# A 352-byte tile at the right-hand end of SBUF moves the right-hand pools from 480 to 128 bytes over multiples of 512

## The chip, the cores and the metric

The kernel runs on one core of a Trainium2 chip. The metric is the device time of one execution in microseconds. Before the change three runs took 923.97, 925.14 and 925.65 us, median 925.14. All durations below are from one profiled execution, which took 923.92 us.

## The reference

A linear attention with a decaying state, then two feed-forward nets. What is computed, cut short:

```python
B, H, S, D = 4, 8, 768, 48
for t in range(S):
    cur = einsum('bhd,bhe->bhde', u * k[:, :, t], v[:, :, t])
    y[:, :, t] = einsum('bhd,bhde->bhe', r[:, :, t], state + cur)
    state = w * state + einsum('bhd,bhe->bhde', k[:, :, t], v[:, :, t])
x = y as (3072 tokens, 384)
g = x @ w_gate                              # 384 x 1536
x = (g * sigmoid(g) * (x @ w_val)) @ w_out  # back to 384
h = x @ w_in                                # 384 x 2048
out = (h * tanh(softplus(h))) @ w_out2      # back to 384
```

All of it is in float32.

## The kernel before

**Work and stages.** The 768 steps of time are cut into six chunks j of 128, and a chunk holds 4 batches x 128 = 512 tokens: the width of a matmul. Attention of a chunk gives its x, transposed (features on partitions). Then comes the first net, chunk by chunk: 12 blocks f of 128 hidden features; a *unit* is one (j, f). Chunks 0 and 1 are worked in pairs for the first seven f. Attention of the later chunks is done in small matmuls between the units of the chunk before. The second net runs after that over three pairs p of chunks, with a Strassen-like scheme: in each of 8 steps q, 11 products ("regions") of the inputs named b, t and d with weight tiles w_split, and products of the hidden g with weight tiles v in three passes a, b and c.

**Every large product is split.** An operand in float32 is held as a rounded part hi and the rest lo, and `product` (line 287) issues three matmuls of 512 columns on line 290 with the same result tile:

```python
add(0, hi, start, False)      # weight hi, streamed hi
add(0, lo, False, False)      # weight hi, streamed lo
add(1, hi, False, stop)       # weight lo, streamed hi
```

`lhsT`, the weight tile, is loaded into the array (LDWEIGHTS, the engine PEld of the profile), `rhs` is streamed. A unit of the first net has 18 such matmuls for gate and value (3 feature blocks x 3, twice), in which x_hi or x_lo is streamed against w_split, and 9 for the down product, in which g_hi or g_lo is streamed against w_split. In the second net all ten split inputs b, t, d are streamed against w_split, and g_hi, g_lo against v.

**Pools and places.** Pools are allocated from the left-hand end of SBUF upward, or with `side="right"` from the right-hand end downward. All sizes below are bytes in a partition.

- On the left 16,384 bytes are reserved and four constants take 32 each, so wpool begins at 16,512 = 32 x 512 + 128. w_split tiles have 3,072 bytes, the o, g_hi and g_lo tiles 2,048, so wpool, opool and gpool all lie 128 over multiples of 512. In the second net the b, t, d tiles (tpool) and the v tiles (vpool) are on the left too, at 128 over. Attention's state, scores and rkv_sb lie 0 over.
- On the right are wpool2 (the other w_split tiles), xpool0 and xpool1 (x_hi, x_lo of even and odd chunks), and in the second net gpool2 (g), spool2 (split pairs of g) and vsums. In the built program all of them lie 480 over a multiple of 512.

Which side a weight tile of the first net is on is set by its number n = 3 f + i, with i = 0 for gate, 1 for value, 2 for down (`w_tile`, line 133): n up to 10, and 12 and 13, are in wpool, the rest in wpool2. So gate and value weights of f = 0 to 4 are on the left and those of f = 5 to 11 on the right; down weights of f = 0 to 2 are on the left and of f = 3 to 11 on the right. They stay there for all chunks. Split pairs of the second net go through seven buffers in turn (`split_of`): two in gpool on the left, five in spool2 on the right. In the first pair of chunks the pairs k = 0 and 1 (step q = 0) and 7 are on the left, 2 to 6 on the right.

**Order.** Nothing is planned by a scheduler here: instructions stand in the order in which the code issues them (`manual_schedule`), each engine works its own in order, and tiles are guarded by semaphores.

Of the kernel before, what the change touches and what calls it, by code (L numbers as in the profile page):

```python
# [16 lines left out]
P = 128  # L17
# [62 lines left out]

W_KEPT = 13


@with_exitstack
def tile_decay_attention_then_two_ffns(
# [17 lines left out]
        return ap.bitcast(F32)  # L103


    right = ExitStack()
    wpool = ctx.enter_context(tc.tile_pool(name="wpool", bufs=W_KEPT))
    wpool2 = right.enter_context(
# [1410 lines left out]
```

## Time and profile before

| | before |
|---|---|
| median of 3 runs | 925.14 us (923.97 to 925.65) |
| the profiled execution's own time | 923.92 us |
| its span, first to last instruction | 922.2 us |
| TensorE matmul (PE) busy | 911.9 us, 99% |
| TensorE weight load (PEld) busy | 734.7 us, 80% |
| VectorE (DVE) busy | 613.5 us, 67% |
| ScalarE (ACT) busy | 436.4 us, 47% |
| GpSimd (POOL) busy | 171.2 us, 19% |
| DMA | 164.24 MB, 178 GB/s on average |
| mean granted TensorE clock | 0.998 |

Matmuls overlap in the records: one lasts about 390 ns, but the next begins some 230 ns after it. The step from one start to the next is what a stream of them costs, and it is read from the chain of work (a piece of n matmuls in so many us) or from start times in the timeline. The stages: up to about 40 us loads and attention of the first chunks; 40 to 560 us the first net with attention of the later chunks in between, of which chunks 0 and 1 up to about 160 us; from 560 us the second net.

### The profile page before, as it was taken

The numbers are of one execution on the slowest core, as the hardware profiler recorded it, in microseconds if no ns is written. First come the engines' busy times: TensorE is split into PE (matmuls) and PEld (weight loads), VectorE is DVE, ScalarE is ACT, GpSimd is POOL, SyncE is SP. The second block draws the span as 40 slices with busy tenths as digits, with TensorE's granted clock in tenths as the row PEclk, the third lists the DMA queues.
The fourth block names the chain that finished last, engine by engine and source line by source line (L and its number), as shares of the span: only waits on it lengthen the run. The fifth ranks groups of instructions, "written<-read, shape, count | busy, mean of one in ns | idle before, by whom it ended". The sixth has DMA issues, their size and how long they took to land.

```text
span 922.2 us, 14893 instructions
## 1 busy us (share of the span) xinstructions
PE 911.9 (99%) x5625; PEld 734.7 (80%) x5625; DVE 613.5 (67%) x1108; ACT 436.4 (47%) x867; POOL 171.2 (19%) x162
## 2 busy tenths in 40 slices
PE   9999999999999999999999999999999999999997
PEld 6878877777788778878888888888888888888885
DVE  8898888545778676733324645658876487775586
ACT  6765543323333443321123346656665565655454
POOL 4100202566555555442000100000000000000000
PEclk9999999999999999999999999999999999999999
DMA  8454732435676766540004648967844558545264
GB/s 316 154 148 125 240 91 82 144 104 180 197 217 211 257 204 203 176 151 30 24 34 143 189 149 285 362 231 258 302 162 160 179 168 303 203 164 166 72 195 145
DMA packets 78600, 164.24 MB, mean 178 GB/s; under 512 B 7616, under 2 KB 36672, under 8 KB 78528
## 3 DMA queue, kind: packets, MB, share of 16 engines
q1 hardware_dynamic: 78096, 162.50, 53.5%
q0 software_dynamic: 432, 0.79, 0.5%
q8 instruction: 44, 0.72, 0.3%
q14 instruction: 28, 0.23, 0.1%
HBM read 126.82 MB, written 36.44 MB: 177 GB/s over the span
## 4 chain that ended last, share of the span: by engine, by line
PE 96%; DVE 2%; DMA 1%; issue 0%; ACT 0%; DVEq 0%
PE mm L290 41%; PE acc L290 27%; PE at L290 19%; PE at L579 3%; PE at L530 2%; PE mm L530 1%; PE at L556 1%; PE at L612 1%; PE acc L488 0%; DMA v<-w2c 0%; PE at L548 0%; PE at L652 0%; DVE o L723 0%; DVE g_lo L731 0%; PE acc L398 0%
## 5 line engine op out<-in xcount | busy, mean ns | idle before, releaser
L290 PE MATMUL mm<-x_hi,w_split 128*128 128x512 f32 x858 | 283.6, 396 | 1.0 <-DVE w_split L230 1.0
L290 PEld LDWEIGHTS mm<-x_hi,w_split 128*128 128x128 f32 x858 | 161.0, 188 | 39.2 <-DVE w_split L230 1.5
L290 PE MATMUL mm<-x_lo,w_split 128*128 128x512 f32 x429 | 168.2, 392 | 0.1
L723 DVE TENSOR_TENSOR o<-mm,o 128x512 f32<-128x512 f32 x72 | 49.7, 691 | 149.2 <-PE mm L290 108.7
L290 PE MATMUL acc<-g_hi,w_split 128*128 128x512 f32 x390 | 133.9, 398 | 0.0
L932 DVE TENSOR_TENSOR g_lo<-g,g_hi 128x512 fp32r<-128x512 f32 x158 | 106.5, 688 | 23.2 <-ACT g_hi L1010 22.9
L290 PE MATMUL acc<-g_hi,v 128*128 128x512 f32 x316 | 115.7, 394 | 0.6 <-DMA v<-w2c 0.6
L725 ACT ACTIVATE g_hi<-o 128x512 fp32r<-128x512 f32 x72 | 45.5, 632 | 131.9 <-DVE o L723 131.7
L1010 ACT ACTIVATE g_hi<-g 128x512 fp32r<-128x512 f32 x158 | 95.8, 622 | 20.3 <-PE at L290 14.7
L932 DVE TENSOR_TENSOR g<-g,at 128x512 f32<-128x512 f32 x72 | 49.5, 687 | 75.3 <-PE at L290 41.3
L290 PEld LDWEIGHTS mm<-x_lo,w_split 128*128 128x128 f32 x429 | 80.7, 188 | 17.9 <-DVE x_lo L658 0.4
L290 PEld LDWEIGHTS acc<-g_hi,w_split 128*128 128x128 f32 x390 | 73.3, 188 | 18.0 <-ACT g_hi L725 0.2
L719 ACT ACTIVATE o<-mm 128x512 f32<-128x512 f32 x71 | 42.1, 593 | 88.4 <-PE mm L290 70.6
L1205 ACT ACTIVATE g<-g 128x512 f32<-128x512 f32 x72 | 45.5, 632 | 73.1 <-DVE g L932 72.0
L290 PE MATMUL acc<-g_lo,w_split 128*128 128x512 f32 x195 | 77.4, 397 | 0.3 <-DVE g_lo L731 0.3
L290 PEld LDWEIGHTS acc<-g_hi,v 128*128 128x128 f32 x316 | 59.3, 188 | 14.5 <-ACT g_hi L1010 1.0
L731 DVE TENSOR_TENSOR g_lo<-o,g_hi 128x512 fp32r<-128x512 f32 x72 | 53.0, 736 | 23.7 <-ACT g_hi L725 23.7
L932 DVE TENSOR_TENSOR g<-g 128x512 f32<-128x512 f32 x96 | 64.6, 687 | 1.4 <-ACT g L1205 1.3
L290 PE MATMUL acc<-g_lo,v 128*128 128x512 f32 x158 | 62.3, 395 | 0.0
L290 PE MATMUL at<-g_hi,v 128*128 128x512 f32 x192 | 60.7, 395 | 0.0
L290 PE MATMUL at<-b_hi,w_split 128*128 128x512 f32 x144 | 52.2, 390 | 0.0
L290 PE MATMUL mm<-b_hi,w_split 128*128 128x512 f32 x144 | 52.2, 390 | 0.0
(176 smaller groups left out, 1498.9 us busy)
## 6 DMA issues: line engine op xcount, KB each, us to landing
w_raw<-w SPq DMA_DIRECT2D x68, 384.0 KB, 3.5
w_split<-w2s SPq DMA_DIRECT2D x48, 384.0 KB, 5.0
rkv_sb<-rkv_t SPq DMA_DIRECT2D x16, 768.0 KB, 5.0
v<-w2a SPq DMA_DIRECT2D x24, 512.0 KB, 4.0
v<-w2b SPq DMA_DIRECT2D x24, 512.0 KB, 3.6
w_split<-w2z SPq DMA_DIRECT2D x24, 384.0 KB, 4.8
v<-w2c SPq DMA_DIRECT2D x24, 384.0 KB, 3.9
n_sb<-rk_n SPq DMA_DIRECT2D x16, 384.0 KB, 5.6
```

The lines of the kernel that those rows point to most:

```text
L290: nc.tensor.matmul(acc, lhsT=wt[:, i, sl], rhs=rhs, start=start, stop=stop, skip_group_check=goes_on)
L530: nc.tensor.matmul(ps[g][:, i, :], lhsT=a["k"][q, i, :], rhs=a["r"][q, i, :], start=True, stop=True,)
L556: nc.tensor.matmul(ps[t, h * D : (h + 1) * D], lhsT=scores[h % 2][:, h // 2, t], rhs=a["v"][:, h, :], start=(j == 0 and h == heads[0]), st ...
L579: nc.tensor.matmul(ps[q * QUAD : (q + 1) * QUAD, c, :], lhsT=lhsT, rhs=rhs, start=q not in begun_q, stop=ends[q] == n, skip_group_check=True,)
L612: nc.tensor.matmul(ps[q, i, :], lhsT=a["kn"][:, h, :], rhs=v, start=(h < 2), stop=(h >= H - 2), skip_group_check=True,)
L719: nc.scalar.activation(sg, ps, AF.Silu)
L723: nc.vector.tensor_tensor(out=sg, in0=ps, in1=sg, op=ALU.mult)
L725: nc.scalar.activation(hi, sg, AF.Copy)
L731: eng.tensor_tensor(out=lo, in0=sg, in1=f32(hi), op=ALU.subtract)
L932: nc.vector.tensor_tensor(out=o, in0=a, in1=b, op=op)
L1010: nc.scalar.activation(hi, src, AF.Copy)
L1205: nc.scalar.activation(t, t if src is None else src, AF.Mish)
```

## The change

A pool `edge` is opened first on the right-hand side with one tile of 352 bytes in each partition. No instruction reads or writes it. It stays open to the end.

```diff
 W_KEPT = 13
+
+EDGE = 352
...
+    edge = ctx.enter_context(tc.tile_pool(name="edge", bufs=1, side="right"))
+    edge.tile([P, EDGE], mybir.dt.uint8, name="edge")
     right = ExitStack()
     wpool = ctx.enter_context(tc.tile_pool(name="wpool", bufs=W_KEPT))
     wpool2 = right.enter_context(
```

In the built program every tile of a right-hand pool lies 352 bytes lower than before, so 128 over a multiple of 512 where it was 480 over. Left-hand tiles stay where they are. The instructions of all five engines are the same, in the same order and with the same waits; only the addresses of the right-hand tiles differ.

## Rows read from the trace of the kernel before

**Rows 1.** The page: busy time and share by engine; the chain by engine and line.

```profile
PE 911.9 (99%) x5625; PEld 734.7 (80%) x5625; DVE 613.5 (67%) x1108; ACT 436.4 (47%) x867; POOL 171.2 (19%) x162
...
PE 96%; DVE 2%; DMA 1%; issue 0%; ACT 0%; DVEq 0%
PE mm L290 41%; PE acc L290 27%; PE at L290 19%; PE at L579 3%; PE at L530 2%; PE mm L530 1%; PE at L556 1%; PE at L612 1%; PE acc L488 0%; DMA v<-w2c 0%; PE at L548 0%; PE at L652 0%; DVE o L723 0%; DVE g_lo L731 0%; PE acc L398 0%
```

**Rows 2.** Waits of the matmuls: us in total, times, longest us.

```profile
PE acc L398 <- POOL mask L387: 1.4, 1, 1.4
PE at L612 <- ACT o L755: 1.1, 1, 1.1
PE mm L290 <- DVE w_split L230: 1.0, 1, 1.0
PE at L548 <- PE at L652: 0.8, 1, 0.8
PE acc L290 <- DMA v<-w2c: 0.6, 1, 0.6
PE acc L290 <- DVE g_lo L731: 0.3, 1, 0.3
```

**Rows 3.** Chain in order of time (start us, us, what), first net, chunk 5.

```profile
480.98 4.20 PE mm L290 x18
485.18 2.08 PE acc L290 x9
...
493.55 4.21 PE mm L290 x18
497.76 2.08 PE acc L290 x9
499.84 4.21 PE mm L290 x18
504.05 2.10 PE acc L290 x9
506.15 4.08 PE mm L290 x18
510.23 2.10 PE acc L290 x9
```

**Rows 4.** Windows: length, busy us of each engine, granted clock, DMA share, GB/s.

```profile
480.98:499.84 18.86, 18.86 (x82) 15.21 (x82) 8.64 (x22) 5.85 (x10) 0.00 (x0) 1.00 0.38 126
506.15:530.00 23.85, 23.85 (x106) 19.57 (x105) 15.24 (x35) 8.43 (x15) 2.80 (x3) 1.00 0.69 198
...
51.08:99.33 48.25, 48.25 (x208) 38.88 (x208) 42.90 (x101) 29.50 (x66) 0.00 (x0) 1.00 0.49 138
99.33:130.27 30.94, 30.94 (x136) 25.38 (x136) 27.14 (x57) 15.04 (x29) 5.78 (x4) 1.00 0.58 193
560.00:922.00 362.00, 356.77 (x1549) 290.29 (x1548) 256.36 (x423) 212.66 (x373) 0.00 (x0) 1.00 0.62 207
```

**Rows 5.** Timeline of PE (start us, us, ...), second net, q = 0 and 1.

```profile
579.77 0.39 PE L290 MATMUL acc<-g_hi,v 128*128 128x512 f32 x1
...
589.97 0.40 PE L290 MATMUL acc<-g_hi,v 128*128 128x512 f32 x1
590.20 0.40 PE L290 MATMUL acc<-g_lo,v 128*128 128x512 f32 x1
590.44 0.40 PE L290 MATMUL acc<-g_hi,v 128*128 128x512 f32 x1
590.67 0.39 PE L290 MATMUL at<-b_hi,w_split 128*128 128x512 f32 x1
590.90 0.40 PE L290 MATMUL at<-b_lo,w_split 128*128 128x512 f32 x1
591.13 0.62 PE L290 MATMUL at<-b_hi,w_split 128*128 128x512 f32 x2
...
600.30 0.40 PE L290 MATMUL acc<-g_hi,v 128*128 128x512 f32 x1
```

**Rows 6.** Groups by line, operation and shape: count, busy us, mean ns, idle before.

```profile
L290 PE MATMUL acc<-g_hi,v 128*128 128x512 f32 x316 | 115.7, 394 | 0.6 <-DMA v<-w2c 0.6
L290 PE MATMUL acc<-g_lo,v 128*128 128x512 f32 x158 | 62.3, 395 | 0.0
L290 PE MATMUL at<-g_hi,v 128*128 128x512 f32 x192 | 60.7, 395 | 0.0
L290 PE MATMUL at<-g_lo,v 128*128 128x512 f32 x96 | 38.0, 396 | 0.0
```

**Rows 7.** Chain in order of time, second net, one of the three passes b.

```profile
634.26 22.38 PE at L290 x96
```

**Rows 8.** Chain in order of time, the end of the kernel.

```profile
899.89 8.21 PE acc L290 x36
908.11 0.02 issue
908.12 3.94 DMA v<-w2c
```

**Rows 9.** Tile g_lo: duration ns min/median/max, first and last start us.

```profile
L932 DVE TENSOR_TENSOR g_lo<-g,g_hi x158: 683/687/694, 574.5 to 915.7; 128x512 fp32r<-128x512 f32 x158
```

**Rows 10.** Window of the first 40 us, columns as in rows 4.

```profile
0.00:40.00 40.00, 37.65 (x691) 30.02 (x692) 34.60 (x72) 27.08 (x98) 13.98 (x19) 1.00 0.73 260
```

**Rows 11.** Group of attention's matmuls on line 556: count, busy us, mean ns.

```profile
L556 PE MATMUL at<-w_split,s 128*64 128x48 f32 x256 | 9.1, 223 | 0.0
```

## The prediction

> **What bounds the kernel now.** I read the page's busy times and its chain of work first [rows 1]: TensorE has a matmul in flight for 911.9 of 922.2 us, and 96% of the chain that ended last lies on it, 87% of it in the three groups of line 290, the split matmuls of the two feed-forward nets. Next the waits of TensorE [rows 2]: six of them, 5.2 us together. So the time is, to a few microseconds, the number of matmuls on line 290 times the step from one to the next, and an edit counts for what it does to that step. No instruction is added or moved, so the question is whether the step depends on where the operands lie.
>
> The chain in order of time answers it [rows 3]. A unit of the first net is 18 matmuls for gate and value (activations x streamed against a weight tile) and 9 for the down product (g streamed against a weight tile). In chunk 5 the 18 take 4.20 to 4.21 us in the units up to 499.84 us and 4.08 us from 506.15 us on: 233.8 against 226.7 ns a step. What changes there is the place of the weight tiles: for f = 0 to 4 gate and value weights are in wpool, 128 over a multiple of 512; from f = 5 on in wpool2, 480 over. x is in a right-hand pool, at 480, all the time. So the pair on **unlike** places (480 with 128) is slow and the pair on **like** places (480 with 480) fast. The granted clock does not tell the two apart: it is 1.00, the 2.4 GHz level, in every stretch looked at [rows 4].
>
> The second net gives the control, with like pairs at 128, the very place that the change gives to all [rows 5]. There the weights (w_split, v) are always at 128. Of seven split buffers of g in turn, two are in gpool, at 128, and five in spool2, at 480. From 579.77 us, q = 0 with g at 128: the next such place is at 589.97 us, 45 matmuls in 10.20 us, 226.7 ns. From 589.97 us, q = 1 with g at 480: 45 matmuls to 600.30 us, 10.33 us. Inside it the steps with g are 230 to 240 ns (589.97, 590.20, 590.44, 590.67), and the first steps after them 230 too (590.67, 590.90, 591.13): what an unlike pair costs trails on for a few like ones. That also reads the down products of the first net: g at 128 with a weight at 128 (f = 0 to 2) takes 2.08 us for nine, between two unlike groups, and with a weight at 480 it takes 2.09 to 2.10 [rows 3], where nine like steps would be 9 x 226.7 ns = 2.04 us.
>
> **The change part by part.** *The tile itself*: no engine writes or reads it, no instruction goes with it; cost nothing. *The move by 352 bytes*: wpool2, xpool0 and xpool1, later gpool2, spool2 and vsums go from 480 to 128. After it x, g, the weights, v and the t, b, d operands of line 290 are all at 128.
>
> First net: 72 units, 12 in each of six chunks. The 30 with f up to 4 go from 4.21 + 2.08 = 6.29 us to 4.08 + 2.04 = 6.12, 0.17 each: 5.1 us. The 42 others go from 4.08 + 2.10 = 6.18 to 6.12: 2.5 us. Sum 7.6 us, all of it on the path, since TensorE is the chain there.
>
> Second net: 762 matmuls stream a split g [rows 6]: 316 + 158 + 192 + 96. The three stretches of 96 (pass b) take 22.38 us each [rows 7], 21.76 at 226.7 ns: 0.62 us, 6.5 ns for each of the 96; at that rate all 762 give 4.9 us. By the other piece, 0.13 us for the 12 unlike ones in 45, trail included, 10.8 ns each on 5/7 of 762 = 544: 5.9 us. I take 5.2, nearer to the first, which has 288 of the 762 under it.
>
> Together 12.8 us. Not all of it arrives. After a stop for the small attention matmuls the first steps are slow whatever the places, and at the very end the last load of v is chained to TensorE: 3.94 us of DMA from the last buffer's release, of which 0.6 us is a wait [rows 2, 8]; matmuls that cover it and get shorter by 3% leave 0.1 us more. I put what is left over at 0.8 us and **take 12.0 us** off.
>
> *The other engines.* VectorE and ScalarE read and write the moved tiles too. The 158 subtractions that make the g_lo of the second net, five in seven of them with all tiles at 480 and two in seven with the split pair at 128, all lie within 683 to 694 ns [rows 9], so the place costs them nothing either way. *The start*: before 40 us the attention matmuls on the w_split inputs read the moved tiles against the scores, which stay at 0 over. A 480/0 pair becomes a 128/0 pair; the trace has no such pair. Priced from both sides by the nearest row, 7.1 ns on 256 matmuls [rows 10, 11] is 1.8 us more or less, of which little is on the path, since VectorE is busy for 34.60 of those 40 us. I take 0 and keep half of that for the range.
>
> The sum is made against the profiled execution, 923.92 us: 911.9. It lies 1.2 us under the median of the runs, 925.14, so the forecast for the median is 925.1 - 12.0 = **913.1 us**.
>
> *A rule that speaks against it.* The rows say that the step is 7 ns longer where the streamed operand and the weights lie on unlike places [rows 3, 5]. The Trainium skill, page "TensorE: Matmul & The Clock Gate", section "Part 2: What happens when you issue a matmul", says that TensorE has two independent SBUF read ports and that "Loading the next tile's weights doesn't steal SBUF read bandwidth from the running matmul"; by that the place of one against the other could not matter and the time would stay at 925.1. The trace does not agree, 4.21 against 4.08 us for 18 matmuls; what is left of that rule is the second rival.
>
> **The rivals.** *1. Waits take part of it back.* VectorE is busy for 42.90 of 48.25 us between 51 and 99 us and for 27.14 of 30.94 up to 130 us, where it splits the weights, and for 256 of 362 us in the second net [rows 4]. If a 2 to 3% faster TensorE runs into it, the 14 units up to 130 us give back 8 x 0.17 + 6 x 0.06 = 1.7 us and the second net, at worst half of its 5.2, 2.6 us: 12.8 - 4.3 = 8.5 off, 916.6. Against it: in these stretches the chain still lies on TensorE, with 5 and 4 us of VectorE idle against 1.4 and 0.3 saved.
>
> *2. Nothing happens.* The step goes with something else that changes at the same f or q, not with the places: 925.1. Against it: the jump is at f = 5 for the 18, in the other direction for the down products, and in the second net between neighbouring q.
>
> *3. The like pair at 128 does not settle in the first net.* There the only like pair at 128 runs at 2.08 us for nine, not 2.04 [rows 3]. If that is no trail but the pace of this stage, 72 x 0.04 = 2.9 us stay, and about 1 us of the trails in the second net: 12.0 - 3.9 = 8.1, 917.0.
>
> *4. Slower: in the first net an operand at 128 is what is slow, whatever its partner.* All rows of that net allow it: 480/128, 128/480 and 128/128 are slow there, and only 480/480 fast. Then the 42 groups of 18 that now take 4.08 us go to 4.21, 42 x 0.13 = 5.5 us, nothing is won in this net, and if the g of the second net gain nothing either the time is 930.6. It decides from f = 5 on: whether the 18 take 4.08 or 4.21. Against it: b, t and g at 128 run at 226.7 ns in the second net, with the same kind of weight tile.
>
> *5. The tile does not move the pools.* Excluded as far as the build shows: the addresses are 352 lower and all other things alike.
>
> **How the numbers follow.** Forecast 0.80; waits 0.07, 916.6; not settled 0.06, 917.0; nothing 0.045; slower 0.025. The range holds the forecast, with 925.1 - 13.5 - 0.9 = 910.7 at its lower end (nothing lost, the highest of the two prices for the second net, and the start going the good way), and the two part gains: 910.7 to 917.4. About 0.2%, 1.9 us, is what a measurement of this kernel can tell from no change. Faster by more: 0.93; within: 0.045; slower: 0.025.
>
> **What would show it.** In the chain of the changed kernel every undisturbed group of 18 should be 4.08 us, for f below 5 too, the down products 2.04 for nine, the 96 of pass b 21.8 us. The TensorE waits should stay near 5 us and the durations of VectorE and ScalarE as they are; the waits of TensorE on VectorE would grow in rival 1. Groups of 4.21 from f = 5 on are rival 4, an unchanged pattern is rival 2, nine in 2.08 everywhere rival 3.

## The result: 912.9 us, and the profile after

The changed kernel takes 912.93 us (median of four runs, 912.33 to 913.93), the kernel before beside it 924.85. The ratio is 0.9872 with a 95% interval of 0.9855 to 0.9890. The forecast was 913.1.

The page of the changed kernel, busy time by engine, and the two of the six waits of the matmuls that grew (us in total, times, longest; line numbers are four higher than before):

```profile
PE 901.0 (99%) x5625; PEld 734.6 (81%) x5625; DVE 611.5 (67%) x1108; ACT 435.9 (48%) x867; POOL 174.1 (19%) x162
...
PE mm L294 <- DVE w_split L234: 1.3, 1, 1.3
...
PE acc L294 <- DMA v<-w2c: 0.8, 1, 0.8
```

Against [rows 1] TensorE lost 10.9 us of busy time with the same 5,625 matmuls, and against [rows 2] the six waits grew from 5.2 to 5.6 us, no more. The chain of the changed kernel in chunk 5 (start us, us, what), then a pass b of the second net, answering to [rows 3] and [rows 7]:

```profile
482.78 4.08 PE mm L294 x18
486.86 2.04 PE acc L294 x9
...
507.26 4.08 PE mm L294 x18
511.34 2.04 PE acc L294 x9
...
628.21 21.76 PE at L294 x96
```

Every undisturbed group of 18 is now 4.08 us, at f below 5 and above, every nine of the down product 2.04, the 96 of pass b 21.76. These are 226.7 ns a step everywhere. The timeline of the second net, where q = 1 took 10.33 us for 45 matmuls [rows 5], has 10.20 from one such place to the next, and the three steps with g are like the rest:

```profile
584.53 0.39 PE L294 MATMUL acc<-g_hi,v 128*128 128x512 f32 x1
584.76 0.39 PE L294 MATMUL acc<-g_lo,v 128*128 128x512 f32 x1
584.98 0.39 PE L294 MATMUL acc<-g_hi,v 128*128 128x512 f32 x1
585.21 0.39 PE L294 MATMUL at<-b_hi,w_split 128*128 128x512 f32 x1
...
594.73 0.39 PE L294 MATMUL acc<-g_hi,v 128*128 128x512 f32 x1
```

### The profile page after: what moved, and what is told of

The parts are those of the page before. It is cut to its first block, busy times and chain, and to the rows that moved or that the text cites. A ratio compares the mean times of both kernels' runs of the same rounds, so it can differ in the third digit from the quotient of the medians.

```text
span 911.7 us, 14893 instructions
## 1 busy us (share of the span) xinstructions
PE 901.0 (99%) x5625; PEld 734.6 (81%) x5625; DVE 611.5 (67%) x1108; ACT 435.9 (48%) x867; POOL 174.1 (19%) x162
## 4 chain that ended last, share of the span: by engine, by line
PE 97%; DVE 2%; DMA 0%; issue 0%; ACT 0%; DVEq 0%; POOL 0%; POOLq 0%
PE mm L294 41%; PE acc L294 26%; PE at L294 19%; PE at L583 3%; PE at L534 2%; PE mm L534 1%; PE at L560 1%; PE at L616 1%; PE acc L402 1%; PE acc L492 0%; DMA v<-w2c 0%; PE at L552 0%; PE at L656 0%; DVE o L727 0%; DVE g_lo L735 0%
## 5 line engine op out<-in xcount | busy, mean ns | idle before, releaser
L294 PE MATMUL acc<-g_hi,w_split 128*128 128x512 f32 x390 | 132.0, 393 | 0.0
```

The lines of the kernel that those rows point to most:

```text
L294: nc.tensor.matmul(acc, lhsT=wt[:, i, sl], rhs=rhs, start=start, stop=stop, skip_group_check=goes_on)
```

## The experiments

**The tile at the other end.** The same tile, opened on the left, so that the left-hand pools go to 480 and the right-hand ones stay there:

```diff
-    edge = ctx.enter_context(tc.tile_pool(name="edge", bufs=1, side="right"))
+    edge = ctx.enter_context(tc.tile_pool(name="edge", bufs=1))
```

> The 352-byte tile at the left-hand end instead of the right: both sides at 480. Theory A (like places): the same gain as the change, 912 to 914 us, groups of 18 at 4.08 us, nine down products at 2.04. Rival C (a place of its own, the good one being 128 for the right-hand pools): 925 us or more, since nothing lies at 128 any more.

Measured 913.35 us, ratio to before 0.9876 (0.9859 to 0.9892). So 128 is not a good place and 480 not a bad one; what counts is that the two sides agree. The chain in chunk 5:

```profile
483.05 4.08 PE mm L294 x18
487.13 2.04 PE acc L294 x9
```

**x alone.** The tile between wpool2 and the x pools, closed with them, so that only x moves to 128:

```diff
+    edge = right.enter_context(tc.tile_pool(name="edge", bufs=1, side="right"))
+    edge.tile([P, EDGE], mybir.dt.uint8, name="edge")
     xpools = [
```

> The 352-byte tile between wpool2 and the x pools, closed with them: x at 128, wpool2 and the second net's right-hand tiles still at 480. Theory A (difference): gate and value of f = 0 to 4 are now alike (4.08 us for 18), of f = 5 to 11 unlike (4.21); down products of f = 3 to 11 stay unlike (2.10). The 42 slow groups and the trails cost more than the 30 of before: 42 units at 4.21 + 2.10, 30 at 4.08 + 2.04 to 2.09: first net about 12 x 0.13 = 1.6 us longer than before, second net as before: 926 to 928 us. Rival C (x at 128 is good by itself): first net as in the changed kernel, 5 to 7 us under before, 918 to 920.

Measured 926.28 us, ratio 1.0018 (1.0009 to 1.0028): slower than before, with x where the change puts it. The chain in chunk 5 is the mirror image of [rows 3]: fast up to f = 4, slow from f = 5, and the second net is as before (22.38 for 96):

```profile
498.71 2.04 PE acc L294 x9
500.75 4.08 PE mm L294 x18
504.83 2.10 PE acc L294 x9
506.93 4.22 PE mm L294 x18
```

The down products of a unit stand behind the gate and value group of the next one, so 498.71 is f = 2 and 504.83 is f = 3. The chain also shows the down products at f up to 2 (128 with 128) at 2.04 us, as soon as their neighbours are like pairs. The 2.08 of [rows 3] was the trail.

**Single matmuls, nothing else at work.** A kernel of its own: runs of 30 matmuls of 512 columns with the streamed operand at one offset and the weights at another, in one tile that begins at a multiple of 512:

```python
a, b = m // 4, (far + w) // 4
nc.tensor.matmul(acc, lhsT=big[:, b : b + P], rhs=big[:, a : a + N], start=True, stop=True)
```

> Leaves out the whole computation: only runs of 30 split-type matmuls of 512 columns, one run for each pair of places of streamed operand and weights (bytes over a multiple of 512), with no other engine at work. Theory A (the difference of the two places sets the step, in a pattern that repeats): runs with streamed operand and weights at the same place step at 226.7 ns, 30 in 6.80 us; 480 with 128 and 128 with 480 at 233 to 235 ns, 30 in 7.0 us; the 16 places of one against 128 for the other fall into a fast and a slow set, the same set whichever of the two is moved, and which set tells the grain: with a grain of 64 bytes every second of the 16 is fast, with a grain of 512 only one is. Distance in steps of 512 (2560 to 16384) changes nothing. Rival B (other engines' traffic on the moved tiles makes the difference, not the pair itself): all runs alike at one step. Rival C (an operand at 128 is slow by itself): 480 with 480 fast, 128 with 128 slow.

Its chain, one piece for each run. From the top: 128 with 128; then the streamed operand at 0, 64, 128, 192, 384, 448 and 480 with weights at 128; then weights at 64 for an operand at 128; last, a like pair with the weights 16,384 further on.

```profile
23.64 6.80 PE qb L43 x30
30.44 6.99 PE qc L43 x30
...
44.46 7.00 PE qe L43 x30
...
58.46 6.83 PE qg L43 x30
...
72.28 6.87 PE qb L43 x30
...
114.18 6.83 PE qa L43 x30
...
128.01 6.87 PE qc L43 x30
134.88 7.01 PE qd L43 x30
...
155.85 6.88 PE qg L43 x30
...
315.35 6.80 PE qb L43 x30
```

Like pairs step at 6.80 / 30 = 226.7 ns (6.83 with the trail of the run before), the other multiples of 32 bytes at 232 to 234. The pattern repeats after 256 bytes, not 512: 384 is as good as 128, 448 as 192. One place is half good: an operand 64 above its weights, 6.87 to 6.88 us or 229 ns. The other way round, 64 below, it is not (7.00). There is no other engine's traffic in this kernel, so rival B, and any story of DMA or VectorE in the way, falls. A grain of 64 bytes falls too, and so does rival C: 128 with 128 is fast. At the end the kernel also alternates, with one operand always at 128 and the other at 128 and 480 in turn: 30 matmuls take 6.90 us, whichever of the two alternates, half-way between 6.80 and 7.00.

**Other sizes of the tile in the kernel.** The change itself with `EDGE = 96` (right-hand pools at 384), `EDGE = 288` (192) and `EDGE = 320` (160).

> The tile at the right-hand end with 96 bytes: right-hand pools at 384, a difference of 256 to the left-hand ones. Theory of a 256-byte pattern (from the runs of single matmuls): as fast as the changed kernel, 912 to 914 us, 18 in 4.08 us and nine in 2.04. Theory that like means the same place in 512: as slow as before, 924 to 926.

Measured 913.09 us, ratio 0.9877 (0.9862 to 0.9892): the period of 256 bytes holds in the kernel.

> The tile with 288 bytes: right-hand pools at 192, 64 above the left-hand ones. By the runs of single matmuls a streamed operand 64 above its weights steps at 229 ns, one 64 below them at 233: gate and value of f = 0 to 4 at 4.12 us for 18, down products of f = 3 to 11 at 2.10 as before, pass b of the second net near 21.9 us. 30 units x 0.11 = 3.3 us and 3.6 of 5.2 in the second net: 917 to 919 us. If only a multiple of 256 counts and all else is alike: 924 to 925. If a grain of 64 bytes is enough: 913.

Measured 923.00 us, ratio 0.9987 (0.9977 to 0.9997). The expectation, 917 to 919, failed. Its chain in chunk 5, with the gate and value group, the down products behind it, and a group of right-hand weights, then pass b:

```profile
486.76 4.14 PE mm L294 x18
490.90 2.08 PE acc L294 x9
...
505.41 4.10 PE mm L294 x18
...
633.78 22.20 PE at L294 x96
```

4.12 was expected for the first, 4.08 for the third, 21.9 for the last; the down products here (f = 1) are a like pair and carry a trail, 2.08. The 229 ns of the half-good place is a pace that a long run of one kind settles to. In the kernel the kinds change every 3 to 18 matmuls, and like groups took 4.10, where before they took 4.08. By the chain the first net gave 1.2 us, and the second net, where 3.6 were expected, lost 0.3: outside pass b the first three stretches of 45 matmuls with g at 192 took 10.35, 10.40 and 10.36 us, before 10.32, 10.34 and 10.27. That the trails of these changes ate the gain is argued from such sizes; no run took them apart.

> The tile with 320 bytes: right-hand pools at 160, 32 above the left-hand ones, for a tile nearly as large as that of the change. By the runs of single matmuls all unlike pairs step at 233 ns: 924 to 926 us, the chain as before. If the tile or the lower addresses as such made the kernel faster: near 913.

Measured 925.08 us, ratio 1.0007 (0.9997 to 1.0016): a tile nearly as large brings nothing. Neither the tile nor the lower addresses as such are the cause.

**Which weights, which widths, which grain.** A second kernel of single matmuls, with alternating pairs, 16-byte offsets and narrower streams:

```python
[(128, 128, N), (480, 480, N)]    # like its own weights, unlike the next ones
[(128, 480, N), (480, 128, N)]    # unlike its own, like the next ones
```

> Leaves out the whole computation: runs of 30 matmuls again, without other engines. Which weights have to be alike? Two runs tell it: in one the places alternate 128 with 128, 480 with 480, so that a matmul is like its own weights and unlike the next one's; in the other 128 with 480, 480 with 128, so that it is unlike its own and like the next one's. Theory N (what collides with the streaming is the load of the next weights, which the trace shows beside it): the first run steps at 233 ns (7.0 us for 30), the second at 226.7 (6.80). Theory O (a matmul against its own weights): the other way round. Theory I (an operand is good or bad by itself): both alike, near 230. Differences of 16 bytes (odd multiples): if 256 bytes is the whole pattern with one good place, all eight at 230 to 234 ns; one under 226.7 would be a better place than that of the changed kernel. Like pairs at 0, 64, 256 and 480: 226.7 each, if only the difference counts; streamed operand 64 above the weights at four places: 229 each. Widths of 384 and 256 columns: like 384/512 and 256/512 of the step plus a constant, 173 and 120 ns; unlike 5 to 7 ns more if the cost is one collision for each load, in proportion to the width if it is spread over the stream.

The chain: these two runs, then 384 columns like and unlike (480 with 128), 256 columns like and unlike.

```profile
146.96 7.02 PE qf L48 x30
...
160.82 6.90 PE qa L48 x30
...
174.53 5.22 PE qc L48 x30
179.76 5.30 PE qd L48 x30
185.06 3.59 PE qe L48 x30
188.65 3.60 PE qf L48 x30
```

The first run, like its own weights, is slow all the same (234 ns); the second lies between (230, in steps of 224 and 236). So theory O falls. Theory N gets the first run right and the second not. The unlike cost depends on the width: 6.7 ns at 512 columns, some 3 at 384, none at 256. Among the eight 16-byte offsets none is under 226.6; one, 240 bytes above the weights and so 16 below them over multiples of 256, equals a like pair.

**Single events, and bfloat16.** The last kernel puts one odd matmul in ten into a stream of like ones, and repeats the places in bfloat16:

```python
every((128, 480, N), LIKE)               # odd weights
every((480, 128, N), LIKE)               # odd streamed operand
every((480, 480, N), LIKE)               # both odd, in one matmul
every((480, 128, N), (128, 480, N))      # odd stream, then odd weights
```

> Leaves out the whole computation: single odd matmuls in a stream of like ones (128 with 128), one event in ten, 60 matmuls each time; 60 like ones take 13.60 us. Four kinds of event: (1) one matmul with weights at 480; (2) one with the streamed operand at 480; (3) one with both at 480, like in itself, unlike the loads beside it; (4) one with the streamed operand at 480, and the next one's weights at 480: unlike in themselves, but each load beside a stream of its own place. Theory N (a stream collides with the load of the next weights): extra time in 1, 2 and 3, twice as much in 3, none in 4. Theory O (own weights): extra time in 1 and 2, none in 3, twice as much in 4. Theory P (more than one neighbour counts): extra time in all four. From the unlike pairs in the kernel an event with its trail costs some 10 ns, six of them 0.06 us. Widths: unlike against like 448 and 320 columns: if the cost grows from 256 columns on as seen at 384 and 512 (0, 3.3, 6.7 ns), 5.0 and 1.7 ns a step. In bfloat16: if the pattern is one of bytes, 480 and 192 and 160 with 128 slower than 128 with 128 and 384 as fast; if it is one of float32 only, all alike.

The chain: each case with its 60 matmuls (13.60 us if all were like), then in bfloat16 an operand at 128 and at 480 with weights at 128.

```profile
29.70 13.76 PE qc L61 x60
...
50.26 13.80 PE qe L61 x60
...
70.86 13.76 PE qg L61 x60
...
91.42 13.79 PE qb L61 x60
...
139.55 6.47 PE qb L61 x30
146.03 6.47 PE two L61 x30
```

All four kinds cost 0.16 to 0.20 us for six events, 27 to 33 ns for each with its trail, three times the 0.06 us expected. That is theory P: neither the own nor the next weights alone decide it. Which accesses meet inside the engine stays open. In a settled stream each of these odd events costs, but the costs do not add up: with a change of place at every matmul, as in the alternating runs of the first kernel, the step is 230 ns, less than the 233 of unlike pairs that never change. In bfloat16 the step is 6.47 / 30 = 215.8 ns, and the same at 384, 192 and 160: none of the places tried costs anything there. The widths 448 and 320 gave 2.8 and 0.6 ns a step, less than the 5.0 and 1.7 expected; 448 columns cost less than 384 did, so the cost does not grow evenly with the width.

## Why the prediction was right, point by point

**What bounds the kernel**: TensorE's step on line 290, as read. 912.9 against 913.1.

**Like and unlike places**: the mechanism of the forecast. Both sides at 128 (912.9), both at 480 (913.4) and x alone moved (926.3) came out in the order that like and unlike give. What the prediction called the place over a multiple of 512 is finer than that: 256 is the period that counts.

**The terms of the sum.** By the chain the second net gave what was forecast, 5.2 us: from the last down products of the first net to the last long piece it took 908.11 - 547.35 = 360.76 us before and 897.50 - 541.94 = 355.56 after. The first net gave less, 6.1 us (505.19 against 499.05, from the piece of 17 at 42.16 and 42.89 us on) where 7.6 stood in the sum. The chain at the ends of three stretches of the first net, before, and in the second fence after:

```profile
42.16 4.25 PE mm L290 x17
...
163.82 1.67 PE at L579 x56
...
462.32 4.08 PE mm L290 x18
...
547.35 4.38 PE acc L290 x18
```

```profile
42.89 4.16 PE mm L294 x17
...
162.80 1.67 PE at L583 x56
...
458.30 4.08 PE mm L294 x18
...
541.94 4.36 PE acc L294 x18
```

In the last stretch no attention stands between the units, and it gained 1.39 us, just what the sum has for its 14 units (5 x 0.17 + 9 x 0.06). The middle one gained 3.0 us (298.50 against 295.50) where the sum has 15 x 0.17 + 24 x 0.06 = 4.0, and the first 1.75 where it has some 2.2. In the first, 0.3 us of the loss is the wait for the weights that VectorE splits (1.0 to 1.3 us, the first of the waits shown under the result).

The step that was mis-sized is the one that took all 72 units as undisturbed. After attention's small matmuls the stream settles anew whatever the places: in the middle stretch the first ten split matmuls after each such stop start 242.3 ns apart on average before and 241.8 after, all later ones 234.4 and 230.4. The chain before and, in the second fence, after, around two such restarts, one with left-hand and one with right-hand weights:

```profile
234.18 4.40 PE mm L290 x18
...
256.62 4.31 PE mm L290 x18
```

```profile
232.65 4.35 PE mm L294 x18
...
254.76 4.35 PE mm L294 x18
```

One gains 0.05 us instead of 0.13 and the other loses 0.04. The 0.8 us that the prediction set aside for such losses was meant for that and was too little by about 0.7 in this stage. Two smaller things in the working: the 30 units have 2.08 us for every down product where those of f = 3 and 4 take 2.10, 0.2 us too little in the sum, and the upper end of the range, 917.4, stands 0.4 over the higher of the two part gains without a reason.

**The start**, priced at 0 with 0.9 either way: in the profiled execution the 12 warm-up matmuls took 5.30 instead of 4.33 us, and the group of 17 began 0.73 us later. The timeline before, then after:

```profile
1.43 4.33 PE L398 MATMUL acc<-mask 128*128 128x512 bf16 x12 [1.43 <-POOL mask L387]
```

```profile
1.43 5.30 PE L402 MATMUL acc<-mask 128*128 128x512 bf16 x12 [1.43 <-POOL mask L391]
```

These 12 read nothing but the mask, a left-hand tile that the change does not move. Their single starts in the two traces show what differs. Before, they are some 427 ns apart up to the eighth at 4.39 us and 216 ns, half of it, from the ninth at 4.73 us on: the 1.2 GHz level of TensorE's clock, then 2.4 GHz. After, all 12 are some 427 ns apart. (The windows of the profile give a granted clock of 1.00 for the first 6 us of both, but the first record of the clock in the traces is from 4.63 us before and 6.78 us after.) With 320 bytes, where the right-hand tiles moved too, the 12 took 4.21 us again. And the three kernels of single matmuls, whose first 30 matmuls are the same, took 9.95, 9.18 and 9.15 us for these 30. So the length of the warm-up goes with the execution and not with the places.

Attention's matmuls on line 560, which read the moved tiles, take 9.2 us in total, before 9.1 [rows 11]. In the other kernels the group of 17 begins at 42.56 to 43.13 us, whatever their speed (42.58 with x alone moved, 42.78 with 320 bytes). With 320 bytes it does so in spite of the short warm-up; what delayed it there stays open. So the start's part is 0.4 to 1.0 us, with one profile of each kernel. With it the spans differ by 10.5 us (922.2 to 911.7) and the profiled executions by 10.5 (923.92 to 913.44), the medians by 11.9. The profiled execution after lies 0.5 us over its median, the one before some 1 us under its own. Part of the close hit of 12.0 is luck of that kind: the path of the two profiles gave 11.3, without the start.

**The end**: the wait on the last load of v grew from 0.6 to 0.8 us, 0.1 was put down for it.

**The rivals.** *Waits* took back 0.4 us, not 4.3: VectorE had the slack that [rows 4] shows. *Nothing happens* fell, and with it what the prediction drew from the page of the Trainium skill cited there, that the place could not matter: for these operands it does, and in bfloat16 the runs show no cost of place. Whether the load of the next weights takes anything from the running matmul is not decided: theory N, which says so, held in one of its two alternating runs and failed in the single events. *Not settled* fell: nine like products at 128 take 2.04 us in the first net. *Slower* fell at the place where it was to be decided: from f = 5 on the 18 take 4.08 us. *The other engines*: the g_lo subtractions lie within 683 to 694 ns as before [rows 9].

No version beats the changed kernel: 226.7 ns was the floor of the mean step at all float32 places tried, and it is the step everywhere outside the restarts.

## What to carry to other kernels

In a stream of matmuls of 512 columns with float32 operands (tiles of type float32r here), put all streamed operands and all weights on the same place over multiples of 256 bytes, for both ends of the memory if pools grow from both; here it is worth 3% of each matmul that was not. Read it from the chain: groups of equal matmuls whose time per step falls into two levels, and the tiles' addresses beside them. Half-good places that look fine in a long run can lose their gain where kinds of matmul alternate.

## What had not been expected of the hardware

- A float32 step of 512 columns is 226.7 ns at best, a bfloat16 one 215.8. Like steps settle at 173.3 ns with 384 columns, 146.7 with 320 and 120.0 with 256. With the 226.7 of 512 that is 53.3 ns for every 128 columns and a constant of 13.3 ns. Like steps of 448 columns do not lie on this line: 202.7 ns where it gives 200.0.
- An unlike pair costs nothing at 256 columns and 6.7 ns at 512.
- After one odd matmul among like ones the stream needs five or six steps to settle, after a run of unlike ones up to ten. The one odd matmul costs 27 to 33 ns in all, as much as four to five steps of a steady unlike run.
- The cost is not symmetric: an operand 64 bytes above its weights is half good, one 64 bytes below is not.
